# Decoding double-precision weights by one bf16-to-f16 conversion and one shift-or, with a new instruction order

## The chip, the cores and the metric

The kernel runs on one core of one Trainium2 chip. The metric is the device time of one execution in microseconds (us), the median of several runs.

## The reference

Block-causal attention over (4 batches, 8 heads, 576 positions, 64 columns), then two feed-forward layers over the 2304 resulting rows of 512 columns. Cut to what matters:

```python
scores = scale * np.matmul(q, k.transpose(0, 1, 3, 2))
scores = np.where(block_i >= block_j, scores, -1000000000.0)   # blocks of 64
attn = softmax(scores)
x = (attn @ v) as 2304 x 512
h = x @ moe_w_in                    # 512 x 2048
x = (h * np.tanh(softplus(h))) @ moe_w_out
h = np.maximum(x @ moe2_w_in, 0.0)
out = (h * h) @ moe2_w_out
```

The four weight matrices arrive as 8-byte floats (float64): the product of a float32 array and a float64 scale. [...]

## The kernel before

**Tiles and passes.** The 2304 rows are six chunks of 384 (`NX`). Each layer works on one chunk at a time, a *pass*: 16 steps `f`, each with a first matmul group into the PSUM tiles `hp` (L1209), an activation `h` on ScalarE (L1215), a split of `h` into two f16 parts `g` (first part on ScalarE L1034 or GpSimd L1035, second part on VectorE L745), and a second matmul group into `acc` (L1275). Three f16 products stand for one f32 product. The very first pass (layer 0, chunk 0) multiplies f32 numbers directly (L1229, L1244), because the split weights aren't there yet. There are 12 passes; their order is `PASSES`, (layer, chunk): (0,0), (0,1), (0,2), (1,0) and so on.

**Attention** is computed in pieces between the matmuls of the passes: scores on TensorE (L833, and L836 for the mask) into the PSUM tile `spare`, a maximum on VectorE (L843), exponentials on ScalarE that read `spare` (L851, output `pad`), scaled and split into `pb` (L870, L745), transposed by DMA, multiplied with `v` (L931) back into `spare`. The short pieces go through L967, L977, L990 in the same way.

**Weights.** There are 32 units of 128 x 1024 weights, 16 for each layer. `decode` loads one unit as 8-byte integers (L1053, 1 MiB) into one of the buffers `raw`, `pad`, and then works on the two 4-byte words of each number in three kinds of step: ScalarE multiplies the high word, read as f32, by 2^-112 (L1060); VectorE shifts the result left by 3 bits (L1063), puts the sign in (L1064) and puts the top 3 bits of the low word in (L1066). `weigh` squares the unit on ScalarE (L1078) and sums over the partitions on TensorE into a few columns of `spare` (L1081), from which VectorE makes a scale (L1087, L1090, L1029). `split` makes two f16 parts, on ScalarE (L1034) and VectorE (L745), and stores them to HBM (`wspill`), or keeps the first ones in `first`. The results of decode stand in `first`, `late`, `ws` (layer 0) or in the three buffers `wf` (layer 1). Layer 0 is decoded in pass (0,0), layer 1 in passes (0,1) and (0,2); pass (1,0) can't scale its inputs before the last unit of layer 1 is weighed.

**Input scales.** Before each pass its input chunk `xs` is split into `x` (L1158, L1159, L745), squared (L1168), summed on VectorE (L1171, L1172) and on TensorE (L1173, into `hp`).

**Order.** Every operation is recorded as a task of a small scheduler (`Sched`); a string `PLAN` says for each place in the program which task stands there and on which engine it runs, where it has a choice (ScalarE, GpSimd or VectorE). The kernel issues its instructions in that order, and each engine executes its own in order. `opened` and the field `banks` serve only the search that made a `PLAN`: they say how long a PSUM tile is shut to one engine after another has used it. All DMAs are issued from SyncE.

Several tiles in the program are views of one PSUM tile: scores, attention outputs, the sums of `weigh` and the maxima for scales all lie in `spare`.

Of the kernel before, what the change touches and what calls it, by code (L numbers as in the profile page):

```python
# [71 lines left out]
REBIAS = 2.0 ** -112  # L72
# [22 lines left out]
    "RbG<*e9F+nSge_OR{Eg95a}g{kabXd%1P}m$F#rXlWzQeTwayYa<?4T2k_!S-K@i;JF8FXQ0XGiN*S|`+kUIPWPq&I&a#D@|5^UQ`F&-huFw&Z%;&H4Ik{B^"
    "OEX!`{2*y153zbB^QqcYzUHYf_N*;mXdh1d8vA76*A_CARm-%MRFmEMIjfdvN2w~G=}~sx$GvJHd7+kJ-+VOqNcTud`G8fO<wjP$r#H$w`U$$ct#`^oErnec"
    "=uGsP&-0u5KGF2Pu0*R<GFOYrySjoq&Cvn+sm{iJb99l`lf~Lr{z??)GYfUG<dFH2!_3tW**O)z&(l}6i8PS&+T7HW7c?r3&3Ua$)YX(pdaGQ~*Y&hKrN?!O"
    "rV?kb=qvK1p2Jr!==G9Be5Gmwd4?GIiw@J0#Me-r!0N&Jy6lqT=BT#OW^%pMVyv{;gO_&d24eew?vRINootgXx=p_$vQzW{?$8f!7L@OGl=Rl`i2Qs~PTFc7"
    ">8@M#7H-{He$X%EGi-d9b|Al&={jt`o_M;Q+oefCcC5v^Dda^LS*5w9slF*+YBOyl(}-px%e5Xm*UJ=HV4g$ACHjPXsMWNFwwB5A3bqw(&iinpuAE%P4~_6_"
    "C!+2jW+h(ei&w|W*YcLO<Fwaxo=!F&=~9`?$?tI99QJi2R_1798Dk!n8Js`bOw$?qju~YV_}ou=%XD383dvhiMFyKFJ9lB@J~G9O*YdJeCV&H*Ipq%NDql!h"  # L100
    "8AD{3#O`;=Nba1f<IDw_NE|$+BZ<Gf@|YRRX|36pQ$}ll{SRW|oU|~liLjAG)<n~s7#yKprH%~3Ly6K*?v%Goec7y!^8O%rGQ#xIfqEPGG#pFZB)!P+szg?2"
    "Jpd9kl?pNo1Zgbg&3#$~e|04KnqYxHYhSYaHqC1qf_4d<&`ArM=d_d7W^XT|sJ-Sfjr6kSk`6@KFL?D<ZKdVpJ!z%4W8+HP@DlU4Ni(vcJh50p8tcRQ2B_DF"
    "dpDK3Iz<{{??!STF;YVt64!^Mr`92_Zz75-X)Q2Qn5j(MkCC<5WVCiL0&15dZb}f>Wu*jGy;T$SI`Aw}ihyvJh>H^7P=XEzYZH(=L<{K|&Mu_sItXvRh?WoP"
    "^D<jbn({ga?@p2=aI(I>OT<n9@!pn1-KS&ZuTq^z8VlZ3MT5#j@Luva9nFjBqwJXha+P7vA)O{a>SS4MlJrUWgorB!_8kVf{sJz(CKJJhe3D<s%gZtj<eH{C"
    "K=l#C=9A!Ik{vCtuzNB&@|n40XONTMf^8eYz-Q$}{X2O%PG+)e4borJcjP&=*>8uFG2_9!uk>Z2X%zYQj2^I4%`i}Bmp%nvz9i%Iepzo9>Hx6t9@%0S>qanU"
    "kv;`tzCpH5(>CPRaHOoZQ}rz!OuYBk&ut%>&7S9pgIQ>@1pK{|NbD;2o5ebod%cR>x%O2m;Apf<)oF}2r?#{<bL}(wxQ+%pM(J$ZQl8_4o59w0Qr}GH3}Ttx"
    "4}jz?iR1p{?MUq+!*rmjWL_W!hNzFqTZo)zcvX?oW&`;!+%^Gw$6=Q$NE)MqY=5NIA$ISVlIBqzfgF+CrWBR)4!N0~#ic&p`jb44jJu?ZZ6iCh1>WmJ?axcp"
    "m6J`{kBBY@Ql?28TU#od&Qe!OOI6UbgLct|L|RvJtN|z1m2KKVYY^Q9!SUNUwJkNEjA;t1$SH$Bzxq_KRYZ9c>~Jl))(G_Z62$#Qn`l+N7A?M(FS%EJa_CN}"
    "K^CWiFqJreomSTiwi2;im6%Q>&U~h#yw{N%LEYt?n@`IycR_O#>07Zueo&#h{E2Fum-xDg$e#iFe@8|a)Nj<<ZB*H7G><+j7wuR0H3u?Ef;(@3)y3qDwHhU3"
    "F55JlM8;gS<%qrdM1F>SUo-7d#?tL+vS=kpk*cR`5t*r9=@<4#a`8q^ZHo<G12=O}w>MKke%AfAI5=Ml+)mLCv0aAlv>o9|nYzsuphk2tUCmkWVkQ}QTJJP5"  # L110
# [1488 lines left out]
```

## Time and profile before

| | us |
|---|---|
| median of 3 runs | 942.67 |
| lowest and highest | 934.58, 943.7 |
| the profiled execution | 941.45 |
| its span, first to last instruction | 939.4 |

Mean granted TensorE clock in the profiled execution: 0.994 of full speed (2.4 GHz). PE is TensorE, PEld its weight loads, DVE VectorE, ACT ScalarE, POOL GpSimd, SP SyncE. "Idle before, releaser" and the view of waits say for how long an engine had nothing to do and what ended that. Matmuls are pipelined, so the mean duration of one is about twice the distance between two.

### The profile page before, as it was taken

Reading aid. Unit: us, or ns where it says so; the run is one execution under the profiler, and the core shown is the slowest. Engines: PE = TensorE matmul, PEld = TensorE weight load, DVE = VectorE, ACT = ScalarE, POOL = GpSimd, SP = SyncE. Lnnn points to the kernel's source line nnn. Section 1 sums busy time; section 2 is a strip of 40 time slices with the busy share of each in tenths; the row PEclk is TensorE's granted clock in tenths of the full one; section 3 lists DMA queues with packets and bytes.
Section 4 is the critical chain, followed back from the end, with each engine's and each line's share of the span. In section 5 each row is a group of like instructions: output and inputs, shape, how many; then the busy total and the mean of one; then the engine's idle time right before and its main releaser. Section 6 shows DMA issues by size and latency. Waiting matters only on the chain. (4 is left out here: it accounts for less than half of the span.)

```text
span 939.4 us, 15711 instructions
## 1 busy us (share of the span) xinstructions
PE 901.2 (96%) x5786; PEld 532.3 (57%) x5786; DVE 574.7 (61%) x1386; ACT 618.9 (66%) x1177; POOL 82.5 (9%) x114
## 2 busy tenths in 40 slices
...
GB/s 350 293 223 235 206 184 191 183 289 290 245 216 234 199 226 228 193 169 229 195 153 99 113 204 226 164 201 178 199 102 68 68 68 68 112 135 135 168 112 34
DMA packets 141772, 168.79 MB, mean 180 GB/s; under 512 B 105856, under 2 KB 110976, under 8 KB 137600
## 3 DMA queue, kind: packets, MB, share of 16 engines
...
HBM read 125.30 MB, written 17.30 MB: 152 GB/s over the span
## 5 line engine op out<-in xcount | busy, mean ns | idle before, releaser
L745 DVE SCALAR_TENSOR_TENSOR g<-h,cst,g 128x384 f16<-128x384 f32 x176 | 108.0, 617 | 233.5 <-ACT g L1034 222.7
L1215 ACT ACTIVATE h<-hp,cst 128x384 f32<-128x384 f32 x176 | 101.1, 577 | 216.4 <-PE hp L1209 211.1
L1275 PE MATMUL acc<-g,ws 128*128 128x384 f16 x1128 | 229.7, 326 | 2.7 <-DMA ws<-wspill 1.6
L1275 PE MATMUL acc<-g,raw 128*128 128x384 f16 x984 | 204.6, 326 | 0.0
L1209 PE MATMUL hp<-x,first 128*128 128x384 f16 x768 | 157.8, 330 | 3.8 <-ACT h L1215 3.8
L1275 PEld LDWEIGHTS <-ws 128*128 128x128 f16 x1128 | 108.7, 98 | 78.1 <-issue 5.4
L1209 PEld LDWEIGHTS <-first 128*128 128x128 f16 x960 | 92.7, 99 | 70.7 <-issue 13.0
L1275 PEld LDWEIGHTS <-raw 128*128 128x128 f16 x984 | 95.5, 98 | 63.0 <-issue 0.6
L1209 PE MATMUL hp<-x,raw 128*128 128x384 f16 x552 | 117.9, 326 | 0.0
L1209 PE MATMUL hp<-x,ws 128*128 128x384 f16 x408 | 85.0, 328 | 0.0
L1209 PEld LDWEIGHTS <-raw 128*128 128x128 f16 x648 | 61.6, 98 | 41.1 <-issue 2.0
L745 DVE SCALAR_TENSOR_TENSOR pb<-pad,st,pb 128x384 f16<-128x384 f32 (+2 forms) x96 | 72.0, 756 | 20.2 <-ACT pb L870 20.1
L1034 ACT ACTIVATE g<-h,cst 128x384 f16<-128x384 f32 x123 | 75.1, 612 | 13.3 <-PE acc L1275 12.5
L870 ACT ACTIVATE pb<-pad,st 128x384 f16<-128x384 f32 (+2 forms) x96 | 66.7, 711 | 15.0 <-DVE st L863 4.9
L851 ACT ACTIVATE pad<-spare,st,sq 128x448 f32<-128x448 f32 (+1 forms) x96 | 65.2, 680 | 15.8 <-DVE st L846 9.2
L1035 POOL TENSOR_SCALAR g<-h,cst 128x384 f16<-128x384 f32 x53 | 43.1, 815 | 342.5 <-PE acc L1275 129.7
L1209 PEld LDWEIGHTS <-ws 128*128 128x128 f16 x504 | 48.5, 98 | 32.3 <-issue 1.8
L843 DVE TENSOR_REDUCE st<-spare 128x2 f32<-128x896 f32 (+1 forms) x48 | 47.8, 996 | 11.4 <-PE spare L836 9.5
L1229 PE MATMUL hp<-xs,first 128*128 128x384 f32 x128 | 49.5, 495 | 0.1
L1220 ACT ACTIVATE h<-h 128x384 f32<-128x384 f32 x85 | 43.5, 513 | 0.8
L1209 PE MATMUL hp<-late,first 128*128 128x384 f16 x192 | 41.7, 326 | 0.0
L833 PE MATMUL spare<-q 64*128 64x448 f16 (+2 forms) x384 | 39.0, 309 | 2.7 <-ACT pad L851 1.6
...
## 6 DMA issues: line engine op xcount, KB each, us to landing
...
raw<-in_w_dram SPq DMA_DIRECT2D x27, 1024.0 KB, 5.6
...
pad<-in_w_dram SPq DMA_DIRECT2D x5, 1024.0 KB, 5.1
...
```

The costliest lines, as they stand in the source:

```text
L745: return sch.add("DVE", c_dve(n) + 62 * ap, lambda: nc.vector.scalar_tensor_tensor(dst(), a(), s() if ap else s, c(), op0, op1), r=r, w=w, ...
L833: nc.tensor.matmul(out=pp.t[:, hd, o:o + k1 - k0], lhsT=qh.t[rows, u, a:a + 128], rhs=qh.t[rows, w, nq + k0:nq + k1], start=p == 0, stop=p ...
L843: sch.add("DVE", c_dve(2 * (o1 - o0)), lambda: nc.vector.reduce_max(both(st, j, r0), pp.t[r0:, :, o0:o1], axis=AX.X), w=[(pp, 0), (st, j)])
L851: t = sch.add("ACT", c_act(o1 - o0, True, 3), lambda hd=hd: nc.scalar.activation(pf[hd].t[r0:, k0:k0 + o1 - o0], pp.t[r0:, hd, o0:o1], AF. ...
L870: sch.add("ACT", c_act(n, False, 1), lambda pb=pb, pv=pv, s=s: nc.scalar.activation(pb.t[:, 0:i + 1, 0, :], pv(), AF.Copy, scale=s()), r=[ ...
L1034: "ACT": ("ACT", c_act(n, False, 1), lambda: nc.scalar.activation(dst(0), src(), AF.Copy, scale=s()), False),
L1035: "POOL": ("POOL", c_pool(n, False), lambda: nc.gpsimd.tensor_scalar(dst(0), src(), s(), 1.0, ALU.mult, ALU.mult), False),
L1209: nc.tensor.matmul(out=hp.t[:, 0:n], lhsT=w.t[:, f % 2, a, 128 * k:128 * k + 128], rhs=x.t[:, c, k, 0:n], start=k == 0 and i == 0, stop=k ...
L1215: sch.add("ACT", c_act(n, True, 1), lambda: nc.scalar.activation(h.t[:, 0:n], hp.t[:, 0:n], (AF.Mish, AF.Relu)[l], scale=hs()), r=[(cst, ( ...
L1220: "ACT": ("ACT", c_act(n), lambda: nc.scalar.activation(hv(), hv(), AF.Square), False),
L1229: nc.tensor.matmul(out=hp.t[:, 0:n], lhsT=wf.t[:, 512 * (f % 2) + 128 * k:512 * (f % 2) + 128 * k + 128], rhs=xs.t[:, k, 0:n], start=k == ...
L1275: nc.tensor.matmul(out=acc.t[:, 0:n], lhsT=wo.t[:, f % 2, a, 128 * m:128 * m + 128], rhs=g.t[:, c, 0:n], start=f == 0 and i == 0, stop=f = ...
```

## The change

`decode` loads the unit one 16-bit number late: of each row of 4096 such numbers it leaves out the first, so that 4095 (8190 bytes) are moved, from a place in HBM 2 bytes further on. In the buffer the top 16 bits of each 8-byte number are then a bf16 number, and the 32 bits below them one aligned word. ScalarE converts the bf16 number to f16, and its 16 bits are written into the upper half of the 4-byte result; GpSimd has set the whole result to zero before. VectorE shifts the 32-bit word right by 13 and ors it in. Both `TENSOR_SCALAR` L1063 and one `SCALAR_TENSOR_TENSOR` (L1064) are gone. The rules of the order search are changed (any of PE, ACT and DVE shuts a tile to the other two, and `spare` counts as one), and `PLAN` is another one.

```diff
-REBIAS = 2.0 ** -112
...
 PLAN = (
-    "c-p<13B1kay2qb)tz{l#i%q7=nDLlpR^&)U#xkXZGA5-==_t)nk{nVrA*ri_>f{iTkeSGAV{i7(W@Bggzt8>t|L=coyYBtmQ}>>8?bh1=^$ySbywC7^e$QS-"
+    "c-p<13B1kK+Q*;u-+#wEW++33Bszwa44FldDU?~}nS_!d88Tdo(m(?$rMi_uA!WF6O$nKYID}(5$Lu(!y`J~`ANJwa`+0BoecyZS&))mL*Lv1k&w7U6?|JaB"
...
-        others = ("ACT", "DVE") if name == "PE" else ("PE",)
+        others = [o for o in ("PE", "ACT", "DVE") if o != name]
...
-                t.banks = (hd,) if j == 4 else ()
+                t.banks = (0,) if j == 4 else ()
...
-        dma(lambda: nc.sync.dma_start(raw.t, win[l][k, j]), 128 * 8192, w=[raw])
+        dma(lambda: nc.sync.dma_start(raw.t.bitcast(U16)[:, 0:4095], win[l][k, j].bitcast(U16)[:, 1:4096]), 128 * 8192, w=[raw])
         n = 1024
-        words = lambda i: raw.t.bitcast(U32).rearrange("p (c two) -> p c two", two=2)[:, :, i]
-        o = lambda: wf.t.bitcast(U32)
-
-        high = lambda: words(1).bitcast(F32)
+        ends = lambda: raw.t.bitcast(BF16).rearrange("p (c four) -> p c four", four=4)[:, :, 2]
+        mids = lambda: raw.t.bitcast(U32).rearrange("p (c two) -> p c two", two=2)[:, :, 0]
+        high = lambda: wf.t.bitcast(F16).rearrange("p (c two) -> p c two", two=2)[:, :, 1]
+        sch.add("POOL", 1000.0, lambda: nc.gpsimd.memset(wf.t, 0.0), w=[wf])
         choose(ENG["rebias"], {
-            "ACT": ("ACT", c_act(n) + 90.0, lambda: nc.scalar.activation(wf.t, high(), AF.Copy, scale=REBIAS), False),
...
+            "ACT": ("ACT", c_act(n) + 90.0, lambda: nc.scalar.activation(high(), ends(), AF.Copy), False),
...
-        sch.add("DVE", c_dve(n, True), lambda: nc.vector.tensor_scalar(o(), o(), 3, None, ALU.logical_shift_left), w=[wf], lock=True)
         sch.add("DVE", c_dve(n), lambda: nc.vector.scalar_tensor_tensor(
-            o(), words(1), 0x80000000, o(), ALU.bitwise_and, ALU.bitwise_or), r=[raw], w=[wf], lock=True)
-        sch.add("DVE", c_dve(n), lambda: nc.vector.scalar_tensor_tensor(
-            o(), words(0), 29, o(), ALU.logical_shift_right, ALU.bitwise_or), r=[raw], w=[wf], lock=True)
+            U(wf.t), mids(), 13, U(wf.t), ALU.logical_shift_right, ALU.bitwise_or), r=[raw], w=[wf], lock=True)
...
-                    t.banks = (0, 1) if key == "ab" else (1 - inst.idx % 2,) if key == "s1" else (0,)
+                    t.banks = (0,)
```

**First place: TensorE in the first third of pass (0,1), around the second input sum.** Before, a unit's sum into `spare` stands behind the scores of an attention piece (L833 and L836 into `spare`), with one group of first matmuls between them (12 of one kind, one shown):

```order
L833 MATMUL spare<-q_2_1173 128x128
L836 MATMUL spare<-never,above 128x64
L1209 MATMUL hp_132<-x_72,first 128x384
...
L1081 MATMUL spare<-us_1330,onesq 128x1
L1173 MATMUL hp_131<-nsq_1294,ones 128x384
```

Now (the lines are 5 lower there), the sum stands ahead of the scores, and the input sum behind them:

```order
L1076 MATMUL spare<-us_1051,onesq 128x1
L807 MATMUL spare<-sq_1242,ones 128x2
L832 MATMUL spare<-q_2_1148 128x320
...
L835 MATMUL spare<-never,above 128x64
...
L1204 MATMUL hp_132<-x_72,first 128x384
...
L1168 MATMUL hp_131<-nsq_1263,ones 128x384
```

What moved is the unit's sum: it is in `spare` before the scores are, and no longer between them and the exponentials that read them.

**Second place: VectorE beside it,** the rows up to the second half of the input sum (`nsq`) and the read of the unit's sum (`wst`). Before:

```order
L745 SCALAR_TENSOR_TENSOR wn_66<-late,us_838,wn_66 128x1024
L745 SCALAR_TENSOR_TENSOR x_73<-xs_1149,cst_1215,x_73 128x384
L812 TENSOR_SCALAR sq_1274<-sq_1274 128x2
L1196 TENSOR_SCALAR cst_893<-cst_893 128x1
L1087 TENSOR_SCALAR wst_1071<-spare 128x2
L1172 TENSOR_TENSOR nsq_1294<-nsq_1294 128x384
```

Now:

```order
L1166 TENSOR_TENSOR nsq_1263<-nsq_1263,wsq_1292 128x768
L762 TENSOR_SCALAR sv_1079<-sv_1079 128x1
L845 TENSOR_SCALAR st_1300<-st_1300,sq_1060 128x2
L1190 TENSOR_TENSOR cst_868<-cst_868,wst_620 128x1
L1082 TENSOR_SCALAR wst_1319<-spare 128x2
L810 TENSOR_SCALAR sq_1242<-spare 128x2
L1167 TENSOR_TENSOR nsq_1263<-nsq_1263 128x384
```

The read of the unit's sum still stands ahead of `nsq`, but the 1024-wide split that stood with them is elsewhere. In the whole program that read is issued 20 times; with a wait on ScalarE among its waits 7 times before and 2 times now.

**Third place: GpSimd in passes (0,1) and (0,2),** where the clearing of the three buffers `wf` now stands between the first parts of `g`:

```order
L1034 TENSOR_SCALAR g_1507<-h_1463,cst_868 128x384
L1057 MEMSET wf 128x1024
L1034 TENSOR_SCALAR g_1646<-h_1533,cst_868 128x384
L1034 TENSOR_SCALAR g_1675<-h_1630,cst_868 128x384
L1057 MEMSET wf 128x1024
L1034 TENSOR_SCALAR g_1738<-h_1648,cst_868 128x384
L1034 TENSOR_SCALAR g_1786<-h_1721,cst_868 128x384
```

Added are the two rows MEMSET; all 32 such rows of the program are new, and the 16 of layer 0 stand near the program's start.

## Rows read from the trace of the kernel before

**Rows 1.** The page: busy time, share of the span and instructions of each engine.
```profile
PE 901.2 (96%) x5786; PEld 532.3 (57%) x5786; DVE 574.7 (61%) x1386; ACT 618.9 (66%) x1177; POOL 82.5 (9%) x114
```
**Rows 2.** Busy time by stage; columns: us, engines, PEclk, DMA share, GB/s.
```profile
10.00:150.00 140.00, 131.69 (x634) 78.53 (x633) 129.24 (x322) 129.03 (x274) 7.33 (x10) 1.00 0.71 245
150.00:190.00 40.00, 32.60 (x220) 17.77 (x221) 34.98 (x84) 35.47 (x55) 8.16 (x9) 0.91 0.68 184
190.00:330.00 140.00, 131.01 (x894) 75.83 (x892) 127.75 (x296) 122.41 (x199) 18.29 (x23) 0.99 0.79 244
330.00:920.00 590.00, 585.47 (x3932) 345.69 (x3930) 276.42 (x669) 323.45 (x632) 47.68 (x62) 1.00 0.55 152
```
**Rows 3.** TensorE's waits from 10 to 330 us: total, times, longest.
```profile
PE hp L1209 <- ACT h L1215: 3.8, 4, 1.4
PE hp L1173 <- DVE cst L1029: 3.1, 1, 3.1
PE spare L1081 <- ACT pad L851: 1.8, 2, 1.0
PE spare L967 <- ACT pt L977: 1.7, 1, 1.7
PE acc L1275 <- DMA ws<-wspill: 1.6, 1, 1.6
PE spare L833 <- ACT pad L851: 1.6, 3, 1.0
PE spare L931 <- DVE sq L811: 1.1, 1, 1.1
PE acc L1275 <- DVE g L745: 1.0, 1, 1.0
```
**Rows 4.** VectorE's waits from 10 to 330 us, the longest group.
```profile
DVE wst L1087 <- ACT pad L851: 9.9, 6, 3.2
```
**Rows 5.** Timeline of VectorE, 159 us: start, us, what, idle before.
```profile
159.01 0.16 DVE L1087 TENSOR_SCALAR wst<-spare 128x2 uint32<-128x2 uint32 x1 [3.18 <-ACT pad L851]
159.09 0.35 DVE L1172 TENSOR_TENSOR nsq<-nsq 128x384 bf16<-128x384 bf16 x1
```
**Rows 6.** Instructions by line with their shapes: busy us, mean ns, idle before.
```profile
L1063 DVE TENSOR_SCALAR wf<-wf 128x1024 uint32<-128x1024 uint32 x16 | 10.9, 683 | 1.2 <-ACT wf L1060 1.2
L1066 DVE SCALAR_TENSOR_TENSOR wf<-raw,wf 128x1024 uint32<-128x1024 uint32 x16 | 19.5, 1217 | 0.1
L1060 ACT ACTIVATE wf<-raw 128x1024 f32<-128x1024 f32 x16 | 18.4, 1149 | 3.4 <-DVE wf L1066 2.0 <-DVE wn L745 1.2
L1078 ACT ACTIVATE wsq<-wf 128x1024 bf16<-128x1024 f32 x16 | 16.8, 1050 | 2.3 <-DVE wf L1066 2.3
L1034 ACT ACTIVATE g<-h,cst 128x384 f16<-128x384 f32 x123 | 75.1, 612 | 13.3 <-PE acc L1275 12.5 <-ACT h L1215 0.2 <-DVE cst L1198 0.2
L851 ACT ACT_TABLE_LOAD x20 | 25.7, 1283 | 1.1 <-DVE us L1029 0.4 <-DVE cst L1183 0.3
```
**Rows 7.** The same by stage for line L1063 alone (VectorE).
```profile
10.00:150.00 140.00, 13.00 (x19) 1.00 0.71 245
150.00:190.00 40.00, 0.68 (x1) 0.91 0.68 184
190.00:330.00 140.00, 8.20 (x12) 0.99 0.79 244
```
**Rows 8.** GpSimd's instructions by line: busy us, mean ns.
```profile
L962 POOL MEMSET pt<- 128x64 f32 x4 | 0.5, 151 | 0.0
masks.py:197 POOL MEMSET ident<- 128x128 f32 x1 | 0.2, 204 | 0.3 <-POOLq L1580 0.3
```
**Rows 9.** DMA issues: KB each, median us from issue to landing.
```profile
raw<-in_w_dram SPq DMA_DIRECT2D x27, 1024.0 KB, 5.6
```
**Rows 10.** Timeline, 109 to 112 us, GpSimd and VectorE.
```profile
109.25 2.26 POOL L1159 TENSOR_SCALAR x<-xs,cst 128x384 f16<-128x384 f32 x4 [107.65 <-DVE cst L1029]
111.05 1.54 DVE L1064 SCALAR_TENSOR_TENSOR wf<-raw,wf 128x1024 uint32<-128x1024 uint32 x1
```

More of the change, by code (lines that the diff above doesn't have):

```diff
@@ L15 @@
 U32 = mybir.dt.uint32
+U16 = mybir.dt.uint16
 F16 = mybir.dt.float16
@@ L95 @@
[L95 to L110, printed above, removed]
@@ new lines @@
+    "QOz!@1I!J*Q%aa}a!oVJOjAP|nI@7>E@>VaW$rNN)q6c+&S^Heu4lBJxvEz+iC3y7>l~AUT(TNDs`ccYTFokj<)G#;*Yp%}jpc;K$w}R#$MmSSFu8axDra=7"
+    "-e7$e&diKNI@zmT+3Be6*7|Z-x9e{@5dE4<7Wqv#>vc5SBN-&G?9$7+L-uGyib(?cmyIYV?$dITgw!4Kj9IH!^ly^L36A`zTlAzBll$ZfnrG&;4V<-}Q{rT`"
+    "UeaZ<KvyAoSkG!<S&2@`x>5IOeze@nNo$dQPiDyu?q%ex&eMXj9GOj=^}T*5yY)DGxy&c(F0?<df8p+1IP1D5_<Jqomfl_`^|X4@=k<ubCu6a|d)zUZ*Jdnv"
+    "K*u66R6gQ!oi5bXNIff8wTm3m`%EYH954M@6K~pK>$dU&H*U@8r}P@<KEZ8MvDHydA1ps<8`-1>^=CBbE%jvszkAD*@*?t$xpghH{ZX69HeIPzWraS<dj-<p"
@@ new lines @@
+    "YfU-MXD=Bg4P=Sdl@wWpbyn*d?I@k462ErogOVgmwH@zgSa(VirHuT*nqpY;D68&~uAH+{pO^fM6qUQ=YmJw9X3EJIx=7b+OSxOV)xI(pjc=3gQdGXu4|J7$"
+    "sYPU#ey%HIrhdj9^UE5YtGCI=`j+;QX_{9)KyJQ#sIzs7&eE@to~#+<3$gl+c96IA3;9Go!>8Bv6HUQ8ui>>htgIw+^i_RKF6tSgdKOxLA%9VkiTbwQE8~$Z"
+    "VJ_(#+5-DE<(?OGD&88d$K+*f_`FWSL%VdM{z9Z~kvjO~Iq9zj%-ym})?>2~+EaV;?ykAa0b*~fZj?bfNV{oAEhQPvW&E*N+7b=z<r`i_c>knbiSl0ZgzO~R"
+    "y5pD2(m^ZZp|7No9F)bHAakT1vAtd|V6#2aS{iD4`Cc31trjv9nXk>m`i(Y_S6T6mPL^8whK!d3_8oj&MIXXLlcl6Q!|kg`UwHs4_LJe<shO;n=eg-j?Mh~h"
@@ new lines @@
+    "z^<RmFn&!kLy4b~@)maeMyBc@GVTL?S!a^bleC}o5=Y)3tKQbPq`XA2(kLxUWL!i3Ei;0<wkOZxk&Tz9q?Np4#$v~|a;J>ID}|()G?B5|-3&*AMC>z?C`{02"
+    "dDW9&`CXqAM(O~aXd20IZ74mYkM=dQWxVMkgUPv}#85Y_C^h8<78yi7?a<v)g}f}mc)V=ZQl^x6R`0Gq>3#APG2D)9>PSwt)I!8vFC_PY5^dOR1*lg^n(HFu"
+    "w&?>>T4rk#tt=T#BhF}}4NOkXU9XR8dF&?Ag1feps$fJTGTvpkhWaU=wTaKWi1QnIP42-KSIC|zc(S5a<6ecOB9T*>yst$>AJiIBN$)3~^6;IgWr@w|pwD!$"
+    "^&ySdLqugI%_##libh4SXer4|td*2IiRC*O6;o0oyt-*#FtDI@U_7s$z>_)n&c$A-dK)&(q*=AUUgSn`+K16Nd09RJJGv9&tI=ixh&!IR97ne7!dhdbCMUip"
@@ new lines @@
+    "uY(i&^fjp_Dda|i4rARknN7Tml+*eESo$-Ob{P4;koO1mb>_!`(Th2w0K1MN0w<Bn-|JW@fLDh~7s)7Nz?>1x4U+9T5cHZX17M!N$ZI^k%8F0)BYjEM>J%dE"
+    "s-4XVBeDDsI+y5Nqod_bG?)UCB-=#%HkGrN>3n@!I&ju-GmvxU=qMtt2igoaBf!xY^-CQo6J)0yPS$-*_CF`{$iOk|+>bq<kq!10FsQHTCvSkq9}>eqFghFG"
+    "cavqdD;YCVmfB7-1H3jw$9O%b1LRd5!uV8}?GvO2Yfqy6Y2ui1tz`P>3{ZUx=r-64z}9W#80gTJTXX_5dlK<al2hH$wGf#<mHBaaaHr-YGe+y}rjGoAruRt~"
+    "a9|AUdP`ktNKQOTWGx}<hihkUITWO-DJ{vXfzn)>AbZe{wdbX=^wm1j6WnMDQ)b8C<ymoBdh44++CBKYH4%OcfBm4H7->%~RhNQzys|W9u8G!TeIu<crL;Mx"
```

128 lines of the change are left out of this document (63 added, 65 removed).

## The prediction

> **What bounds the kernel now.** I read the page's first part, then the busy time by stage, then the waits of the stage in which TensorE isn't full, then the costs of what is removed. TensorE is busy for 901.2 of 939.4 us [rows 1]; 38.2 us are left, and nothing in the change makes a matmul shorter, so the gain can come only from these and from the clock. The stages say where they lie [rows 2]. From 330 to 920 us TensorE is busy for 585.47 of 590 us: only 4.5 us are to be had, with VectorE and ScalarE half idle. From 10 to 330 us its idle time is 8.3 + 7.4 + 9.0 = 24.7 us. That is the stretch in which weights are decoded, and there the two other engines are nearly as full: VectorE 129.24 of 140, 34.98 of 40, 127.75 of 140 us, that is 292 of 320; ScalarE 129.03 + 35.47 + 122.41 = 287 of 320. The rest of the idle time is the first load, the end, and pieces between. So the first third has three engines near their limit, which wait for each other in turn, and the last two thirds TensorE alone.
>
> The clock adds a little. It is granted at 0.91 of full speed over 150 to 190 us and at 0.99 over 190 to 330 us [rows 2]: 0.09 x 40 + 0.01 x 140 = 5.0 us of full-speed work are lost to stretches at the lower of its two levels (1.2 instead of 2.4 GHz), and the first of these is the stage in which TensorE was idle longest for its length.
>
> Which waits: the eight longest groups of TensorE in that stretch are 15.7 us [rows 3]; the other 9.0 us of the 24.7 are in groups of 0.9 us or less, or named for nothing. Four of the eight concern `spare` and come to 1.8 + 1.7 + 1.6 + 1.1 = 6.2 us. The single longest, 3.1 us, is the input sum L1173 behind VectorE. What held VectorE is seen one step back: it had nothing to do for 3.18 us until 159.01 us, at the read L1087 of a unit's sum from `spare`, which stood ahead of L1172 and waited for ScalarE's exponentials L851, readers of the same PSUM tile [rows 5]. Waits of this one kind are 9.9 us of VectorE in 6 places [rows 4]. The old order was searched with a rule that knew no such wait between ScalarE and VectorE.
>
> **The change, part by part.**
>
> *VectorE's work.* Each unit loses one L1063 (0.683 us) and one of the two 1024-wide shift-ors (the other, L1066, is 1.217 us, and the one left has the same form and width) [rows 6]: 1.90 us. By the counts of L1063 by stage, 19, 1 and 12 [rows 7], that is 36.1, 1.9 and 22.8 us, in all 60.8 us. VectorE's share of the three stages falls from 92, 87 and 91% to about 67, 83 and 75%. It stops being one of the three full engines.
>
> *ScalarE's work.* The conversion stays 1024 wide. It costs between the square L1078, which also writes 16-bit numbers (1.050 us), and the old L1060 (1.149 us) [rows 6]: 0 to 3.2 us less over 32 units. By the order, ScalarE hands 6 first parts of `g` and 3 of `x`, all 384 wide, to GpSimd before pass (1,0), at about 0.61 us each, and loads its function table two times more, at 1.283 us each [rows 6]: 5.5 less and 2.6 more, another 2.9 us less. These are small beside the whole, and I take 0: ScalarE stays at 287 us there, and this caps the gain of the stretch at 320 - 287 = 33 us.
>
> *GpSimd's clearing.* The trace shows 64 and 128 columns, 0.151 and 0.204 us [rows 8]: 0.83 ns a column, so 1024 columns are about 0.204 + 896 x 0.83 ns = 0.95 us, an estimate from these rows; 32 of them are 30 us on an engine that is busy 9% of the span [rows 1]. In layer 0 they stand at the program's start, ahead of any unit. In layer 1 each waits until its `wf` buffer is read out, and first parts of `g` queue behind it, for which TensorE's second matmuls wait. At best this costs nothing, since per unit the chain is 1.90 shorter and 0.95 longer. At worst each of the 12 units of the third stage holds a `g` for its full 0.95 us, 11 us. TensorE has first matmul groups of other steps to do meanwhile, and its wait for `g` is 1.0 us in all now [rows 3]; I take 0.7 us.
>
> *GpSimd beside VectorE.* One shift-or took 1.54 us [rows 10] instead of 1.22 [rows 6], while GpSimd read its inputs: 0.32 us more. At worst all 32 shift-ors meet a clearing, 10.2 us of VectorE, a sixth of what is removed; at best none. I take none, by all the other shift-ors of the same mean [rows 6]. The Trainium skill, SBUF — State Buffer, section Who interferes with whom, says that a VectorE instruction with two inputs in SBUF contends with a GpSimd instruction that reads SBUF, not with one that only writes. The trace agrees in its first half, and no row shows the second; by that rule it is 0, by the stretched row 10.2 us of VectorE's relief, and neither ends on TensorE's path by itself.
>
> *The loads.* Same count, 8190 instead of 8192 bytes a row, and a source 2 bytes off. No load of before does that. Now 1 MiB lands 5.6 us after its issue [rows 9]. I take no change, with the bounds in the third rival. The queue's order moves little.
>
> *The order.* By stage: (a) the wait of 3.1 us at L1173 goes. The unit's sum is now in `spare` ahead of the scores, so its read has no exponentials to wait for; next in line is the next `h`, on ScalarE, which was already done then. -3.1 us. (b) The other waits on `spare`, 6.2 us: half go, because the search now sees them and because VectorE, which makes the maxima that the exponentials need, is no longer full. -3.1 us. (c) TensorE behind ScalarE's `h`, 3.8 us: ScalarE has the same work, so only a third. -1.3 us. (d) The remaining 9.0 us of short waits: a third, -3.0 us. (e) The load of `ws`, 1.6 us, stays, and 1.0 us behind `g` is halved, -0.5 us. (f) Clock: the gaps ahead of the stretch at the lower level shrink by half, and I take half of the 5.0 us back, -2.5 us.
>
> *Sum.* -3.1 - 3.1 - 1.3 - 3.0 - 0.5 - 2.5 + 0.7 = -12.8 us. Against the profiled execution's own 941.45 us this is 928.7 us; that execution lies 1.2 us under the median of 942.67 us, so the forecast is 930 us. ScalarE would then be busy for 287 of 307 us, 93%, which its best stretches already show.
>
> **The rivals.**
>
> *ScalarE becomes the bound.* It has 287 us of work in the 320 us, and the same chain (TensorE, exponentials or `h`, TensorE) holds TensorE for as long as before. For it: the longest groups of TensorE's waits name ScalarE [rows 3]. Against it: ScalarE itself waits for VectorE there, at every read of decode results [rows 6]. Then only the waits named for VectorE shrink (3.1 + 1.1 + 1.0 = 5.2 us, of which half), with 0 to 1 us of clock: about -3 us, 940 us.
>
> *The search gets nearly all.* With VectorE free and whole-tile waits planned around, three quarters of the 24.7 us and of the 5.0 us of clock come back: -22 us, 920 us. Against it: ScalarE would have to be busy for 287 of 298 us, 96%.
>
> *Misaligned loads are slower (the other side).* The DMA engines are busy for 0.71 of 10 to 150 us at 245 GB/s [rows 2], so their full rate is 345 GB/s; one unit is then 3.04 us of all of them, and the 19 units of that stage 57.8 us, against 0.29 x 140 = 40.6 us of free DMA time. The loads may become 1.7 times as slow before the stage is short of DMA. Twice as slow would overflow by 17 us, with nothing left of the gain, since every decode then waits for its data: about 958 + 1 = 960 us. For it: nothing in the trace has such an address. Against it: a row is still one long run. The Trainium skill, DMA: Bandwidth & Descriptors, section How a descriptor splits into AXI transactions, has a run fetched in pieces of 256 bytes from the boundary below its start: an estimate by that page is 32 pieces for 8190 bytes from 2 bytes on as for 8192, hence no loss. No run here shows it yet; it is why this rival has little of the chance.
>
> *GpSimd's queue holds the second matmuls.* The upper bound above, 11 us, against half of the gain: about 947 us. Against it: GpSimd was busy for 18 of 140 us in that stage [rows 2], and will be for some 30.
>
> **How the numbers follow.** The forecast's case 0.53 (own range 922 to 936 us), nearly all of it 0.12, ScalarE's bound 0.21, the loads 0.06, GpSimd's queue 0.08. A run of this kernel tells about 1% from no change: 933.2 to 952.1 us around 942.67. Faster by over 1%: 0.12 and most of the forecast's case, 0.47, make 0.59. Within 1%: the rest of the forecast's case 0.06, ScalarE's 0.21, most of GpSimd's 0.06 make 0.33. Slower: 0.06 + 0.02 = 0.08. The range of 8 in 10 goes from 916 us, inside the second rival, to 943 us, which takes in ScalarE's bound.
>
> **What would show it.** Right: VectorE's busy time by about 60 us lower, its share of 10 to 330 us near 72%; no L1063 and 32 clearings near 0.95 us; conversions of 1.05 to 1.15 us; VectorE's waits at the read of a unit's sum well under 9.9 us; TensorE's idle time from 10 to 330 us near 14 us instead of 24.7, and a granted clock nearer to 1.00 at 150 to 190 us; landings of `raw` near 5.6 us. Wrong: the same idle time with ScalarE as releaser; waits of `g` behind a clearing; landings near 10 us with ScalarE waiting for `raw`; a clearing of several us; or a shift-or well over 1.22 us.

## The result, and the profile after

The changed kernel takes 932.22 us (median of 16 runs, 925.81 to 933.62), the kernel before 941.37 us beside it (16 runs): a ratio of 0.9905, 95% interval 0.9887 to 0.9923, so 9 us faster. The forecast was 930 us. The profiled execution took 933.08 us; its span is 931.3 us. In the rows, lines up to L1028 are one lower than before, from the decode's shift-or on five (L974 is now L973, L1087 is L1082, L1209 is L1204).

The number came out near the forecast, but the profile doesn't show what was forecast. First the page's engine line and the busy time by stage, which answer to [rows 1, 2]:

```profile
PE 896.4 (96%) x5786; PEld 531.7 (57%) x5786; DVE 542.3 (58%) x1330; ACT 602.0 (65%) x1143; POOL 122.9 (13%) x166
```

```profile
core 0: us, PE busy (x) PEld busy (x) DVE busy (x) ACT busy (x) POOL busy (x), PEclk, DMA share, GB/s
...
10.00:150.00 140.00, 127.57 (x583) 77.03 (x581) 108.17 (x277) 129.78 (x272) 14.26 (x19) 0.96 0.71 237
150.00:190.00 40.00, 38.95 (x297) 22.62 (x298) 38.05 (x96) 38.81 (x63) 9.47 (x14) 1.00 0.81 209
190.00:330.00 140.00, 129.41 (x896) 75.18 (x894) 115.15 (x294) 124.13 (x200) 38.28 (x46) 1.00 0.86 258
```

From 150 to 330 us TensorE's idle time has fallen from 16.4 to 11.6 us and the clock is full. From 10 to 150 us it has risen from 8.3 to 12.4 us, and the clock has fallen from 1.00 to 0.96. TensorE's waits from 10 to 330 us (columns as in [rows 3]) say what is new:

```profile
PE acc L989 <- DVE ident L698: 9.2, 1, 9.2
PE spare L930 <- ACT pad L850: 2.6, 2, 1.4
PE spare L1076 <- ACT wsq L1073: 1.6, 2, 1.4
PE hp L1004 <- DVE pt L722: 1.2, 1, 1.2
PE spare L1076 <- ACT pad L850: 1.1, 1, 1.1
PE hp L1204 <- ACT h L1210: 1.0, 4, 0.4
PE hp L1168 <- ACT h L1210: 0.9, 1, 0.9
PE hp L1204 <- DMA ws<-wspill: 0.9, 1, 0.9
PE spare L832 <- ACT pad L850: 0.9, 3, 0.3
```

The old waits shrank as a group; one wait of 9.2 us stands alone at the top. VectorE's timeline from 5 us on, and GpSimd's from the start, show where it comes from:

```profile
5.92 0.56 DVE L971 TENSOR_REDUCE st<-acc 128x2 f32<-128x384 f32 x1 [4.65 <-PE acc L967]
6.39 0.21 DVE L972 TENSOR_REDUCE st<-acc 128x1 f32<-128x64 f32 x1
6.64 9.28 DVE L973 TENSOR_SCALAR st<-st 128x3 f32<-128x3 f32 x1
7.73 8.19 DVE L971 TENSOR_REDUCE st<-acc 128x2 f32<-128x384 f32 x1
8.20 7.72 DVE L972 TENSOR_REDUCE st<-acc 128x1 f32<-128x64 f32 x1
15.98 0.17 DVE L973 TENSOR_SCALAR st<-st 128x3 f32<-128x3 f32 x1
```

```profile
0.87 0.95 POOL L1057 MEMSET late<- 128x1024 f32 x1
...
5.92 2.74 POOL L1057 MEMSET late<- 128x1024 f32 x3
8.60 0.95 POOL L1057 MEMSET ws<- 128x1024 f32 x1
9.50 0.15 POOL L961 MEMSET pt<- 128x64 f32 x1
...
14.94 0.95 POOL L1057 MEMSET first<- 128x1024 f32 x1
```

Fifteen clears of layer 0 and the first of layer 1 wait for nothing, so GpSimd runs them one behind the other from 0.87 to 15.89 us (the sixteenth of layer 0, of a `ws`, starts at 89.5 us). The first two reductions of VectorE beside them take their usual time. The TENSOR_SCALAR on three columns, whose next instance takes 0.17 us, takes 9.28 us and ends at 15.92 us, as the last clear does. The two reductions issued behind it end with it. ScalarE's first exponentials, which need it, start at 16.02 us, and TensorE stands from 10.6 to 19.77 us. It then works at a lower clock: 0.76 is granted from 20 to 30 us, where before had 1.00 over 10 to 150 us [rows 2]:

```profile
10.00:20.00 10.00, 0.82 (x7) 0.68 (x6) 8.69 (x16) 3.98 (x19) 5.89 (x7) 0.73 0.90 347
20.00:30.00 10.00, 9.73 (x57) 8.22 (x57) 5.65 (x29) 7.67 (x32) 0.00 (x0) 0.76 0.41 133
```

The decode itself (groups by line; between the two bars stand busy us and mean ns, behind the second bar the engine's idle time before them):

```profile
L1059 ACT ACTIVATE wf<-raw 128x1024 f16<-128x1024 bf16 x16 | 21.6, 1350 | 0.9 <-POOL wf L1057 0.9
L1061 DVE SCALAR_TENSOR_TENSOR wf<-raw,wf 128x1024 uint32<-128x1024 uint32 x16 | 19.5, 1219 | 1.8 <-ACT wf L1059 1.8
L1057 POOL MEMSET wf<- 128x1024 f32 x16 | 15.2, 952 | 48.9 <-DVE wn L744 42.4 <-DVE cst L1023 4.0 <-DVE sv L763 2.6
```

A clear takes 0.952 us and the shift-or 1.219 us, as forecast; the conversion takes 1.35 us and not 1.05 to 1.15.

### The profile page after: what moved, and what is told of

The parts are those of the page before. It is cut to its first block, busy times and chain, and to the rows that moved or that the text cites. A ratio compares the mean times of both kernels' runs of the same rounds, so it can differ in the third digit from the quotient of the medians.

```text
span 931.3 us, 15656 instructions
## 1 busy us (share of the span) xinstructions
PE 896.4 (96%) x5786; PEld 531.7 (57%) x5786; DVE 542.3 (58%) x1330; ACT 602.0 (65%) x1143; POOL 122.9 (13%) x166
## 5 line engine op out<-in xcount | busy, mean ns | idle before, releaser
L744 DVE SCALAR_TENSOR_TENSOR g<-h,cst,g 128x384 f16<-128x384 f32 x176 | 110.5, 629 | 237.8 <-ACT g L1033 226.1
L1204 PE MATMUL hp<-x,first 128*128 128x384 f16 x768 | 156.5, 326 | 1.8 <-ACT h L1210 1.0
L1204 PEld LDWEIGHTS <-first 128*128 128x128 f16 x960 | 92.4, 98 | 63.8 <-issue 4.4
L1204 PE MATMUL hp<-x,raw 128*128 128x384 f16 x552 | 117.5, 326 | 0.0
L1204 PEld LDWEIGHTS <-raw 128*128 128x128 f16 x648 | 61.8, 98 | 41.2 <-issue 1.9
L744 DVE SCALAR_TENSOR_TENSOR pb<-pad,st,pb 128x512 f16<-128x512 f32 (+2 forms) x96 | 72.2, 757 | 22.1 <-ACT pb L869 22.1
L1204 PE MATMUL hp<-x,ws 128*128 128x384 f16 x408 | 83.8, 326 | 0.9 <-DMA ws<-wspill 0.9
L1033 ACT ACTIVATE g<-h,cst 128x384 f16<-128x384 f32 x116 | 70.9, 613 | 12.5 <-PE acc L1270 9.9
L1034 POOL TENSOR_SCALAR g<-h,cst 128x384 f16<-128x384 f32 x60 | 45.0, 752 | 228.9 <-DVE cst L1148 81.1
L1204 PEld LDWEIGHTS <-ws 128*128 128x128 f16 x504 | 47.8, 98 | 31.4 <-DMA ws<-wspill 1.0
L1204 PE MATMUL hp<-late,first 128*128 128x384 f16 x192 | 41.5, 326 | 0.0
L1215 ACT ACTIVATE h<-h 128x384 f32<-128x384 f32 x78 | 39.8, 513 | 0.8
```

Of the source, the lines that this page charges most:

```text
L744: return sch.add("DVE", c_dve(n) + 62 * ap, lambda: nc.vector.scalar_tensor_tensor(dst(), a(), s() if ap else s, c(), op0, op1), r=r, w=w, ...
L1033: "ACT": ("ACT", c_act(n, False, 1), lambda: nc.scalar.activation(dst(0), src(), AF.Copy, scale=s()), False),
L1034: "POOL": ("POOL", c_pool(n, False), lambda: nc.gpsimd.tensor_scalar(dst(0), src(), s(), 1.0, ALU.mult, ALU.mult), False),
L1204: nc.tensor.matmul(out=hp.t[:, 0:n], lhsT=w.t[:, f % 2, a, 128 * k:128 * k + 128], rhs=x.t[:, c, k, 0:n], start=k == 0 and i == 0, stop=k ...
L1215: "ACT": ("ACT", c_act(n), lambda: nc.scalar.activation(hv(), hv(), AF.Square), False),
```

## The experiments

The theory after this reading (A): order and lighter decode are worth some 20 us together, and the burst of clears takes about half of it back. The rivals: the time lost at the start is hidden later (B), or the order, or the decode, is the whole of it (C to E).

**Clears spread.** Each clear that stood at the start, except the very first, now stands in GpSimd's queue ahead of the conversion of the unit before its own, behind a copy of one column that needs that unit's loaded `raw` (`units` lists the units in order, with their buffers, clear `c` and conversion `conv`):

```diff
+    def gated(raw, wf):
+        nc.gpsimd.tensor_copy(wf.t.bitcast(F16)[:, 0:1], raw.t.bitcast(BF16)[:, 2:3])
+        nc.gpsimd.memset(wf.t, 0.0)
+    for (_, raw, _, _, conv), (_, _, wf, c, _) in zip(units, units[1:]):
+        seq.remove(c)
+        seq.insert(seq.index(conv), c)
+        c.fn = lambda raw=raw, wf=wf: gated(raw, wf)
```

> The changed kernel, with the clears of layer 0 (and the first of layer 1) no longer at the program's start: each stands in GpSimd's queue ahead of the conversion of the unit before it, behind a one-column copy from that unit's `raw`, so it can't run before that load has landed. Theory A (the burst of 16 clears holds VectorE's TENSOR_SCALAR L973 for 9.28 us, and TensorE loses 9.2 us of waiting and some of its clock by it): L973 takes 0.17 us again, ScalarE's first exponentials start near 7 us instead of 16, the 9.2 us before the first `acc` matmuls are gone, and the time is 918 to 923 us against 932.2 for the changed kernel. Rival B (the stretch to 330 us is bounded by ScalarE or by the loads, so the time lost at the start is hidden later): L973 short, but the time 928 us or more.

Measured: 924.47 us (4 runs, 921.33 to 925.82) against 942.21, ratio 0.9805 (0.977 to 0.9841). L973's first instance takes 0.17 us, and the stages read:

```profile
10.00:150.00 140.00, 134.79 (x669) 81.33 (x668) 112.49 (x309) 137.15 (x274) 30.90 (x49) 1.00 0.73 242
150.00:190.00 40.00, 38.99 (x275) 22.43 (x273) 37.07 (x75) 39.12 (x62) 9.38 (x13) 1.00 0.99 279
190.00:330.00 140.00, 132.55 (x920) 77.17 (x920) 113.35 (x287) 121.52 (x203) 40.59 (x49) 1.00 0.88 257
```

TensorE's idle time from 10 to 330 us is 5.21 + 1.01 + 7.45 = 13.7 us, the clock is 1.00 throughout. The burst cost about 8 us of median (932.22 less 924.47); B falls. The time is 1.5 us above A's range, which took the whole stall as lost.

In this run single clears meet single instructions, which shows what a clear holds. VectorE's timeline at 24 and 31 us, with GpSimd's clears at those times:

```profile
23.95 1.01 DVE L751 TENSOR_SCALAR pt<-pt,st 128x64 f32<-128x64 f32 x1
24.09 0.88 DVE L973 TENSOR_SCALAR st<-st 128x3 f32<-128x3 f32 x1
...
31.61 1.23 DVE L1064 SCALAR_TENSOR_TENSOR late<-raw,late 128x1024 uint32<-128x1024 uint32 x1
```

```profile
23.96 0.95 POOL L1501 MEMSET late<- 128x1024 f32 x1
...
31.71 0.95 POOL L1501 MEMSET late<- 128x1024 f32 x1
```

The two TENSOR_SCALARs, else of 0.24 and 0.17 us, end 0.05 us behind the clear's end at 24.91 us; the shift-or (L1064 here), which reads two operands, isn't lengthened by a clear that lies wholly inside it.

**The burst in the old kernel**, on buffers that are written later anyway:

```diff
     with tc.manual_schedule():
+        for wf in burst:
+            nc.gpsimd.memset(wf.t, 0.0)
         for t in seq:
```

> The kernel before, with 16 clears of 128x1024 on GpSimd put at the program's start, on buffers that are written later anyway; nothing else. Theory A: VectorE's first TENSOR_SCALAR (L974, 0.17 us) is held until the clears end near 16 us, and the time rises by 8 to 13 us, to 949 to 954 us. Rival B (the start has slack): L974 is held, but the time stays within 3 us of 941.4. Rival F (the stall in the changed kernel has another cause than the clears): L974 takes 0.17 us, and the time is that of before.

Measured: 953.63 us against 942.21, ratio 1.0118 (1.008 to 1.0156), 11.4 us more. VectorE's row and TensorE's new longest wait:

```profile
6.68 9.24 DVE L974 TENSOR_SCALAR st<-st 128x3 f32<-128x3 f32 x1
```

```profile
PE acc L990 <- DVE st L980: 8.9, 1, 8.9
```

The stall stands in the old kernel as in the new, with nothing of the new decode in it. B and F fall.

**The same burst in 64 short clears:**

```diff
-            nc.gpsimd.memset(wf.t, 0.0)
+            for i in range(4):
+                nc.gpsimd.memset(wf.t[:, 256 * i:256 * i + 256], 0.0)
```

> The kernel before with the same burst at its start cut into 64 clears of 128x256 instead of 16 of 128x1024. Theory S (VectorE's TENSOR_SCALAR can't start as long as clears stand in GpSimd's queue without a gap, whatever their length): L974 is held until the last clear, near 16 to 20 us, and the time is 949 us or more as with the 16 long ones. Rival T (it is held for the one clear that runs when it comes up): L974 under 1 us and the time within 3 us of 941 to 942.

Measured: 954.99 us against 940.83, ratio 1.015 (1.0109 to 1.0191). VectorE's row, and the end of GpSimd's queue:

```profile
6.76 11.08 DVE L974 TENSOR_SCALAR st<-st 128x3 f32<-128x3 f32 x1
```

```profile
0.87 0.32 POOL L1505 MEMSET first<- 128x256 f32 x1
...
16.40 1.07 POOL L1505 MEMSET ws<- 128x256 f32 x4
17.41 0.41 POOL L962 MEMSET pt<- 128x64 f32 x4
```

L974 ends at 17.84 us, as the last entry of GpSimd's queue does (17.82), after more than 40 short instructions had begun and ended beside it. So the length of one clear doesn't decide. T falls. In all three bursts a clear begins some 0.06 us before the end of the one ahead of it (0.95 us long and 0.89 apart, 0.32 long and 0.25 apart), so that no gap is left between them. The run with each clear done twice, further down, shows what a gap does.

**The parts alone.** The new order with the old decode, its three VectorE instructions at the place of the one:

```diff
-        sch.add("DVE", c_dve(n), lambda: nc.vector.scalar_tensor_tensor(
-            U(wf.t), mids(), 13, U(wf.t), ALU.logical_shift_right, ALU.bitwise_or), r=[raw], w=[wf], lock=True)
+        sch.add("DVE", c_dve(n), bits, r=[raw], w=[wf], lock=True)
```

(`bits` issues the old shift and both old shift-ors.)

> The new order with the old decode: no clears, aligned loads, the conversion with the scale of 2 to the power -112, and a shift and two shift-ors on VectorE directly behind each other at the place of the new shift-or. Theory A (the -9 us are a gain of some 20 us by order and lighter decode together, less the stall at the start): VectorE busy again for about 603 us, no stall at the start; the planned order is worth something by itself, 930 to 938 us. Rival C (the order is only good with the lighter decode, since each shift-or now comes 1.9 us later than planned for): 941 us or more. Rival D (the order does it all): 925 us or less.

Measured: 973.1 us against 942.21, ratio 1.0321 (1.0283 to 1.0358). VectorE is busy for 593.4 us, and TensorE's idle time from 10 to 330 us is 21.2 + 1.9 + 20.1 us. C holds, more strongly than expected: by itself this order costs 30.9 us, and it is no gain that could have been had without the lighter decode. (An order searched for the old decode with the same rules wasn't tried.)

The old order with the new decode. Its clears of layer 0 stand ahead of the conversion of the unit before, as in the spread version, most of those of layer 1 directly ahead of their own conversion:

```diff
-            "ACT": ("ACT", c_act(n) + 90.0, lambda: nc.scalar.activation(wf.t, high(), AF.Copy, scale=REBIAS), False),
+            "ACT": ("ACT", c_act(n) + 90.0, convert, False),
...
-        sch.add("DVE", c_dve(n, True), lambda: nc.vector.tensor_scalar(o(), o(), 3, None, ALU.logical_shift_left), w=[wf], lock=True)
+        sch.add("DVE", c_dve(n, True), lambda: None, w=[wf], lock=True)
```

(`convert` is the new conversion; the first shift-or goes in the same way, the second becomes the new one, and the load is the shifted one.)

> The old order with the new decode (shifted load, clear, one conversion, one shift-or), its clears behind the loads as in the spread version, so that no burst stands at the start. Theory A: VectorE busy for about 543 us; the wait of 3.1 us at the unit's input sum and the reads of `spare` behind exponentials stay, as the order sets them, while waits named for VectorE shrink: 932 to 938 us. Rival D (the order does it all): within 2 us of 941.4. Rival E (the lighter decode does it all): 925 us or less.

Measured: 945.23 us (10 runs) against 942.21, ratio 1.0043 (1.0017 to 1.0068): slightly slower, which no theory had. ScalarE's waits up to 330 us tell why:

```profile
ACT wf L1061 <- POOL wf L1508: 8.2, 7, 1.9
...
ACT first L1061 <- POOL first L1508: 2.2, 1, 2.2
```

The old order has no place for a clear, and ScalarE waited for 10.4 us behind clears; its conversions are dearer besides. How much each of the two took wasn't parted. To see the relief without both:

```diff
-            "ACT": ("ACT", c_act(n) + 90.0, lambda: nc.scalar.activation(wf.t, high(), AF.Copy, scale=REBIAS), False),
+            "ACT": ("ACT", c_act(n) + 90.0, lambda: nc.scalar.activation(wf.t, high(), AF.Copy, scale=2.0 ** -6), False),
...
-        sch.add("DVE", c_dve(n, True), lambda: nc.vector.tensor_scalar(o(), o(), 3, None, ALU.logical_shift_left), w=[wf], lock=True)
-        sch.add("DVE", c_dve(n), lambda: nc.vector.scalar_tensor_tensor(
-            o(), words(1), 0x80000000, o(), ALU.bitwise_and, ALU.bitwise_or), r=[raw], w=[wf], lock=True)
```

> The kernel before, old order and aligned loads, old conversion on ScalarE (its scale changed so that the numbers stay of ordinary size), with the shift and the first shift-or of every unit left out, so the weights are not the reference's: VectorE is relieved of 1.90 us in each of 32 units and nothing is added. Theory G (the old order's waits are set by the order and by ScalarE, so VectorE's relief alone is worth little): 937 to 942 us against 941 to 942. Rival H (the relief by itself is worth much, and in the run with the old order and the new decode it was eaten by conversions of 1.36 instead of 1.15 us and by the clears): 935 us or less.

Measured: 933.25 us against 941.44, ratio 0.9909 (0.9886 to 0.9931). H holds: relief by itself is worth 8.2 us. The same decode in the new order, where `bits` of the run with the order alone keeps only its last instruction:

```diff
-            nc.vector.tensor_scalar(o(), o(), 3, None, ALU.logical_shift_left)
-            nc.vector.scalar_tensor_tensor(o(), words(1), 0x80000000, o(), ALU.bitwise_and, ALU.bitwise_or)
             nc.vector.scalar_tensor_tensor(o(), words(0), 29, o(), ALU.logical_shift_right, ALU.bitwise_or)
```

> The new order with the lightest decode: aligned loads, ScalarE's old conversion (1.14 us, its scale changed so that the numbers stay of ordinary size), one shift-or per unit, no clears; the shift and the first shift-or are left out, so the weights are not the reference's. It is to the run with the relief alone (933.2 us, old order) what the new order adds, and to the spread version (924.5 us) what the clears and the dearer conversions (1.35 us) still cost there. Theory P (order and relief each give some 8 us, and the clears and conversions cost the rest): 915 to 920 us. Rival Q (in the new order the clears and conversions are hidden): within 2 us of 924.5. Rival R (the order gives nothing that relief doesn't): 930 us or more.

Measured: 919.31 us against 940.83, ratio 0.9766 (0.9732 to 0.9799). P holds. With each run taken against the kernel before beside it, the account is: relief -8.2; the new order on top of it -21.5 + 8.2 = -13.3; clears and dearer conversions -17.7 + 21.5 = +3.8; the burst -9.2 + 17.7 = +8.5; together -9.2 us. The steps are differences of neighbouring runs, so they add up by their making, and by the intervals of the ratios each is known to 2 to 5 us only. The smallest, +3.8, isn't clear of that by itself, but this run and the last one below, taken beside the same runs of the kernel before, differ by 3.1 us, and no run of the one lies in the range of the other (918.31 to 920.53, 921.57 to 923.8).

**What the rest costs.** Each clear done twice in the spread version:

```diff
         nc.gpsimd.memset(wf.t, 0.0)
+        nc.gpsimd.memset(wf.t, 0.0)
```

> The spread version with every clear done twice, back to back: 32 more of 0.95 us on GpSimd, 30 us of its time. Theory N (spread clears cost only the TENSOR_SCALARs of VectorE that they hold, and these have slack): 924 to 928 us. Rival O (first parts of `g` and `x` behind a clear in GpSimd's queue, or the shift-ors beside it, cost the time): 930 us or more, with TensorE's waits for `g` grown by over 2 us, or shift-ors over 1.3 us.

Measured: 928.25 us against 941.44, ratio 0.9864 (0.9849 to 0.9879): about 4 us more than the spread version, between the two ranges. The shift-or still takes 1.218 us, and TensorE's waits for `g` and for `x` behind GpSimd grew by 0.2 and 0.5 us only (0.7 to 0.9, 0.2 to 0.7), so O's causes explain little of it. VectorE's busy time grew by 5.8 us (535.9 to 541.7), and ScalarE waits longer for the clears of `wf`. Its wait in the spread version, and here:

```profile
ACT wf L1062 <- POOL wf L1059: 0.9, 1, 0.9
```

```profile
ACT wf L1062 <- POOL wf L1059: 3.1, 3, 1.9
```

So the clears have a price also when spread, and most of the 3.8 us above may be theirs. Clears and conversions weren't parted.

This run also shows where a stall ends. The second clear of a pair waits for the first and begins 0.06 us behind its end. GpSimd's first pair, and VectorE beside it:

```profile
12.98 0.95 POOL L1501 MEMSET late<- 128x1024 f32 x1
13.99 0.95 POOL L1502 MEMSET late<- 128x1024 f32 x1
```

```profile
13.02 0.94 DVE L979 TENSOR_SCALAR st<-st 128x3 f32<-128x3 f32 x1 [0.53 <-ACT pt L976]
```

L979, else of 0.16 us, ends at 13.96 us, between the two clears. At every later pair that holds a TENSOR_SCALAR, it gets in at the end of the first clear as well: a gap of 0.06 us between clears is enough. Nor does every queue without a gap hold it to the end. In the kernel before, beside the four TENSOR_SCALARs that GpSimd runs without a gap from 109.25 to 111.51 us [rows 10], VectorE has:

```profile
110.39 0.59 DVE L846 TENSOR_SCALAR st<-st,sq 128x2 f32<-128x2 f32 x1
```

It usually takes 0.24 us, and it ends at 110.98 us, behind the third of the four. So the long stall is shown for clears that follow each other without a gap, and not for any busy GpSimd; why those let nothing in stays open.

Aligned loads in the spread version:

```diff
-        dma(lambda: nc.sync.dma_start(raw.t.bitcast(U16)[:, 0:4095], win[l][k, j].bitcast(U16)[:, 1:4096]), 128 * 8192, w=[raw])
+        dma(lambda: nc.sync.dma_start(raw.t, win[l][k, j]), 128 * 8192, w=[raw])
```

> The spread version with whole, aligned loads of `raw` in place of the rows shifted by 2 bytes; the conversion takes the fourth 16-bit word of each number and the shift-or the lower 32-bit word, so the lowest bits of the decoded weights are others (all the work is done, on the same sizes). Theory L (shifted loads cost nothing that counts): within 2 us of the spread version's 924.5 us, with the same conversions of 1.35 us and landings within 0.5 us of its own. Rival M (the shifted address is dearer): landings fall by 0.5 us or more and the time by 2 us or more.

Measured: 923.65 us against 941.44, ratio 0.9816 (0.9798 to 0.9834): the same as the spread version. `raw` lands in 6.5 us there and in 6.1 us with shifted rows. L holds.

Forms of the conversion, and single loads, behind the end of the kernel before (`w(1)` is the upper 32-bit word, `e(3)` and `e(2)` the 16-bit word, `h` the strided and `d` the dense result):

```diff
+            for i in range(4):
+                nc.sync.dma_start(raw, src)
+                nc.scalar.activation(wf, w(1), AF.Copy, scale=2.0 ** -6)
+                nc.scalar.activation(h, w(1), AF.Copy, scale=2.0 ** -6)
+                nc.scalar.activation(d, w(1), AF.Copy, scale=2.0 ** -6)
...
+                nc.sync.dma_start(raw.bitcast(U16)[:, 0:4095], src.bitcast(U16)[:, 1:4096])
+                nc.scalar.activation(wf, e(2), AF.Copy)
+                nc.scalar.activation(h, e(2), AF.Copy)
```

> The kernel before with a tail behind its end: four times a whole, aligned load of `raw` and then a load with rows shifted by 2 bytes, each alone on the queue, and behind each ScalarE conversions of 1024 columns in forms that differ by one thing: 32-bit or 16-bit numbers read with a stride of 8 bytes, and written as 32-bit numbers, as 16-bit numbers 4 bytes apart, or as 16-bit numbers next to each other. If reading 16-bit numbers makes the new conversion dearer, every form that reads them takes about 1.35 us; if writing 16-bit numbers 4 bytes apart does, only these take 1.35 us and the others 1.05 to 1.15 us. If a shifted row costs nothing, both loads land within 0.2 us of each other.

Groups of ScalarE behind the kernel's end. L1512 to L1514 read 32-bit numbers, L1515 to L1517 16-bit ones, after an aligned load; L1519 and L1520 16-bit ones after a shifted one. Of each three, the first writes 32-bit numbers, the second 16-bit ones 4 bytes apart, the third 16-bit ones next to each other:

```profile
L1516 ACT ACTIVATE wf<-raw 128x1024 f16<-128x1024 bf16 x4 | 5.4, 1343 | 0.1
L1520 ACT ACTIVATE wf<-raw 128x1024 f16<-128x1024 bf16 x4 | 5.4, 1343 | 0.1
L1513 ACT ACTIVATE wf<-raw 128x1024 f16<-128x1024 f32 x4 | 5.4, 1342 | 0.1
L1515 ACT ACTIVATE wf<-raw 128x1024 f32<-128x1024 bf16 x4 | 4.5, 1122 | 0.1
L1519 ACT ACTIVATE wf<-raw 128x1024 f32<-128x1024 bf16 x4 | 4.5, 1120 | 20.1 <-DMA raw<-in_w_dram 20.1
L1512 ACT ACTIVATE wf<-raw 128x1024 f32<-128x1024 f32 x4 | 4.5, 1120 | 20.9 <-DMA raw<-in_w_dram 20.9
L1517 ACT ACTIVATE wf<-raw 128x1024 f16<-128x1024 bf16 x4 | 4.4, 1107 | 0.1
```

What is read makes no difference. Writing 16-bit numbers 4 bytes apart costs 0.22 to 0.24 us more for 1024 columns. The waits for four shifted loads sum to 20.1 us, for four aligned ones to 20.9 us, of which the first, behind the kernel's last output, is 6.1 us: about 5 us either way.

**Early clears, then spread.** In the spread version, the clears of the first nine units moved into the time before VectorE has scores to read, five on GpSimd and four on VectorE:

```diff
+    for i in range(9):
+        seq.remove(units[i][3])
+        seq.insert(i, units[i][3])
+        if i >= 5:
+            units[i][3].fn = lambda wf=units[i][2]: nc.vector.memset(wf.t, 0.0)
-    for (_, raw, _, _, conv), (_, _, wf, c, _) in zip(units, units[1:]):
+    for (_, raw, _, _, conv), (_, _, wf, c, _) in zip(units[8:], units[9:]):
```

> The spread version with the clears of its first nine units in the time before VectorE's first work on the scores at 5.9 us: five on GpSimd, four on VectorE; the other seven of layer 0 spread as before. If the TENSOR_SCALARs held by single clears (0.9 to 1.0 us each) still cost TensorE something in the first 60 us, the time is 921 to 923.5 us; if they are hidden, 924 to 925; if VectorE's or GpSimd's early clears run into the first scores, more than 926.

Measured: 922.43 us (4 runs) against 940.83, ratio 0.9799 (0.9766 to 0.9833). It can't be told from the spread version, whose interval it shares, so whether the TENSOR_SCALARs held by single clears cost TensorE anything stays open. Both versions are faster than the changed kernel.

## Why the prediction came out near, and where it was wrong

The forecast was -12.8 us and the result is -9.2 us, but by errors against each other. The burst, +8.5 us, was left out; the other clears and the conversions cost 3.8 us where the sum had 0.7; and order and relief were worth 21.5 us where it had 13.5. The difference, 8.5 + 3.1 - 8.0 = 3.6 us, is small by chance.

*The failed step* is "I take none" under "GpSimd beside VectorE", together with "In layer 0 they stand at the program's start, ahead of any unit", which was costed at nothing. The prediction weighed the clears against the shift-or alone, and there it was right: 1.22 us beside a clear. The Trainium skill, SBUF — State Buffer, section Who interferes with whom, names in the same list what was overlooked: a `tensor_scalar` of VectorE can run in a mode that takes the port pair it shares with GpSimd, and then the one that comes second is blocked for as long as the other's instruction lasts. The traces agree for a single clear (1.01 instead of 0.24 us). For the burst they show more than that: 9.28 and 11.08 us, across many instructions. The trace of before held a sign of it: the L846 of 0.59 us shown above lies in the stretch of [rows 10], from which only GpSimd's instructions and the shift-or were read. No unit's decode was near those clears, but the attention's first scores were; that GpSimd's queue had nothing in it to wait for could be read from the order.

*VectorE's relief.* The removed instructions sum to 61 us, as forecast. VectorE's busy time fell by 52.7 us where nothing else changed (522.0 in the run with the relief alone), since the records of neighbours overlap: taking these 64 out of the trace of before leaves 52.8 us less. In the spread version it fell by 38.8 us: the new order gives VectorE more copies, and TENSOR_SCALARs wait beside clears. Its share of 10 to 330 us is 82%, not 72%, also because the faster kernel does more of its work in that window.

*ScalarE's work.* Taken as unchanged, with conversions of 1.05 to 1.15 us. They take 1.35, since the result is written 4 bytes apart, which the rows of before didn't show: 32 x 0.2 = 6.4 us more. From 10 to 330 us ScalarE is busy for 292.7 us, and for 297.8 in the spread version (93%), where the prediction had 287. Its busy time in the whole fell all the same, from 618.9 to 602.0 us: it loads its function table 42 times instead of 48, and 7 first parts of `g` and 5 of `x` are handed over. The two loads more that the prediction counted before pass (1,0) are there (39 instead of 37 up to 330 us); behind, which it didn't look at, there are 3 instead of 11.

*The order's terms* are read from the changed kernel's waits, without the 9.2. (a) Right: the 3.1 us at the input sum are gone, though the next `h`, taken as done, now holds it for 0.9 us (L1168), and VectorE's waits at the read of a unit's sum behind exponentials fell from 9.9 to 1.1 us. (b) Wrong in its sum: of the four groups two are gone and the others fell to 1.1 and 0.9 us, but L930 behind `pad` grew from 0.9 to 2.6 us and L1076 behind `wsq`, 1.6 us, is new, so the four longest again sum to 6.2 us. (c) Too small: the wait of the first matmuls behind `h` fell by 2.8 us, not 1.3, and with L1168's 0.9 us counted in, by 1.9. (d) Too small: the idle time from 10 to 330 us is 24.1 us; without the 9.2 and the eight next groups (10.2) 4.7 us are left of 9.0. (e) About right: `ws` 0.9 instead of 1.6, `g` 0.6 instead of 1.0 us. (f) Too small where it was looked for: the spread version has its whole clock back, about 5 us instead of 2.5; the changed kernel has it back over 150 to 330 us but loses some over 10 to 150 us (0.96), after the stall. (g) The wait for `g` behind clears, 0.7 us, isn't seen at TensorE; what clears hold outside the burst are ScalarE's conversions (0.9 us of waiting) and VectorE's TENSOR_SCALARs.

TensorE's idle time near 14 us, which the prediction named as its sign, is what the spread version has (13.7). The burst hid it.

*The rivals.* ScalarE as the bound: no, it is busy for 137 of 140 us in the spread version's first stage and TensorE for 134.8 all the same. Nearly all (920 us): this is what order and relief give without clears and dearer conversions (919.3 us). Misaligned loads: no cost; `raw` lands after 6.2 us in the changed kernel instead of 5.6, but after 6.5 us with aligned loads in the spread version. GpSimd's queue: it held something, but VectorE, not the second matmuls.
